# Retention attention and SwiGLU block on one core: first gate weight asked for ahead of the third pair's v, and first gate products ahead of the fourth pair's transposes

## The chip, the cores and the metric

The kernel runs on one core of a Trainium2 chip. The metric is the device time of one execution in microseconds (us). Three runs of the kernel before are shown, with their median. One more execution was profiled; its trace gives every duration used here, and the times in it count from the start of its span.

The engines are named as in the profile: PE (matrix products; PEld is its weight load), DVE (vector), ACT (scalar, activations), POOL (GpSimd) and SP, which here only asks for transfers. A "q" behind a name (SPq) is the sequencer of that engine.

## The reference

```python
def _attn_ref(q, k, v):                       # (8, 8, 576, 64): batch, head, position, head size
    scores = scale * np.matmul(q, k.transpose(0, 1, 3, 2))
    Dmat = np.where(rel >= 0, gamma[:, None, None] ** rel[None, :, :], 0.0)
    return np.matmul(scores * Dmat[None], v)

def _moe_ref(x, w_gate, w_val, w_out):        # x: (4608, 512), d_ff = 1536
    g = x @ w_gate
    return (g * (1.0 / (1.0 + np.exp(-g))) * (x @ w_val)) @ w_out
```

The attention's output, with the heads side by side, is x. All is in 32-bit floats on the chip; the three weights arrive as 64-bit floats.

## The kernel before, in words

**Attention by pairs.** Two heads of one batch are a pair, so there are 32 pairs; pairs 0 to 3 are the first batch. A pair is worked in chunks of 64 positions. Its steps are functions: `transposes` (line 455: PE turns k into `bankC` and q into `bankE`, ACT copies both out at line 467, and for pairs 2 and 3 POOL scales k at line 490), `scores` (547), `new_states` (522: products of k and v by chunk), `masked` (561: a list of ACT's copy `copies`, DVE's mask `own`, and the DVE steps `pairs`, `odd`, `evens` that add up the states), `own_values` (509), `earlier_values` (531: products of states and q, behind an empty instruction that waits for `own_values`) and `to_x` (598: for the first batch three ACT copies at line 625). `new_pair(i)` (777) is `scores`, `new_states`, and all of `masked`. `go_on(n)` and `part_on()` (839, 844) issue the next entries of `masked`.

**The first tile of tokens.** The first 512 positions of batch 0 make a first tile, `xs[0]`, with one group of 128 columns ("c") for each pair. `up0(f, chunks, parts)` (859) multiplies column block f of the weights (gate is part 0, value is part 1; f goes from 0 to 11) by the columns c of the tile. Blocks with an even f use `bankA` and `bankB`, those with an odd f `bankC` and `bankE`; when the last c is in, ACT applies Silu to the gate bank (line 874) and DVE multiplies (line 875), and only then may the bank be written for block f + 2. A product with c = 0 needs pair 0's output, c = 1 that of pair 1, and so on.

**The weights** come in 18 pieces. `load_w(m)` (368) asks for piece m; pieces 0 and 1 (first gate and first value piece) are asked for in halves of two transfers each, 256 KB a transfer. Pieces 0 to 4 are asked for on SP's queue, later ones (1024 KB each) on POOL's. `split(j)` (389) is two ACT instructions that take a half apart (lines 398 and 399), `rounding(j)` (408) two DVE instructions that put it together as 32-bit floats (lines 415 and 416). `split` asks for a later piece when its place comes free, so that POOL's transfers wait for ACT's line 399.

**The order** of each engine's work is written out by hand: the calls at the end of the kernel are the order of every queue. SP asks for transfers one after the other; each transfer uses one of eight semaphores in turn and waits for the one that had the same semaphore before. In the order before, SP asks for pair 2's q, k and v (`load(2)()`, line 325: v is what the second call asks for), then for the first half of the first gate and value piece (line 421), pair 3 (line 422), the second halves, pieces 2 and 3, and piece 4 when `held` is emptied. Then come the loads of pairs 4 and on, line 290 (k, v) and line 299 (eight transfers of 72 KB each of 128-byte rows, for q and k), one pair ahead of their use. From pair 4 on, q and k are turned by DVE at line 477, and ACT scales k at line 492.

Before `up0(0, [0], [0])`, the first gate product, stand 22 products of an identity matrix (line 1461) whose result nobody reads. Before them PE has `new_pair(2)` and `own_values(1)`; after it `earlier_values(1)`, the transposes of pair 3, and the products of c = 1 and of the value part.

## Time and profile before

| | us |
|---|---|
| three runs, median (lowest to highest) | 1014.41 (1012.95 to 1018.09) |
| the profiled execution's own time | 1013.87 |
| its span | 1012.2 |
| PE busy | 1005.7 (99%) |
| DVE busy | 713.4 (70%) |
| POOL busy | 571.9 (57%) |
| ACT busy | 286.4 (28%) |
| 16 DMA engines, mean of the core | 192 GB/s |

The rows of the profile read "start, duration, engine, line, operation, written tile<-read tiles"; in square brackets stands the idle time of the engine ahead of the row and what ended it. A matrix product in 32-bit floats is recorded as two passes, so that 22 products show as x44. [...] The chain of waits is followed back from the last instruction: at each step to whatever released it.

### The profile page before, as it was taken

How to read it: one execution, taken by the hardware profiler on the slowest of the kernel's cores; microseconds unless marked ns; L12 is line 12 of the kernel's file. 1: busy time of each engine (PE TensorE's matmuls, PEld its weight loads, DVE VectorE, ACT ScalarE, POOL GpSimd, SP SyncE). 2: the span in 40 equal slices, each digit the busy share in tenths (PEclk: the TensorE clock that was granted, in tenths of full speed). 3: DMA queues.
4: the chain of work that ended last, by engine and by line, in shares of the span. 5: the costliest groups of instructions: out<-in, count | busy, mean ns of one | idle time of the engine just before them, and what ended most of it. 6: DMA issues, size and time to landing. Idle time of an engine off the chain costs nothing.

```text
span 1012.2 us, 21328 instructions
## 1 busy us (share of the span) xinstructions
PE 1005.7 (99%) x8338; PEld 829.4 (82%) x8338; DVE 713.4 (70%) x1203; ACT 286.4 (28%) x636; POOL 571.9 (57%) x603
## 2 busy tenths in 40 slices
PE   9999999999999999999999999999999999999998
PEld 7655555888888888888888888888888888888887
DVE  5567988677875766977777678866575767566645
ACT  4644622131423312133322202233320012233110
POOL 3510458979475228575565157746672586566514
PEclk9999999999999999999999999999999999999999
DMA  9999986888788887757668686434454554445553
GB/s 242 280 265 258 201 236 230 222 236 217 182 209 215 215 213 215 195 157 197 180 183 225 176 203 197 152 131 161 162 173 141 154 189 147 146 155 184 179 161 103
DMA packets 273932, 194.44 MB, mean 192 GB/s; under 512 B 212328, under 2 KB 241896, under 8 KB 273832
## 3 DMA queue, kind: packets, MB, share of 16 engines
q1 hardware_dynamic: 248296, 94.77, 38.6%
q10 hardware_dynamic: 21360, 84.29, 25.5%
q0 software_dynamic: 4176, 14.03, 4.3%
q8 instruction: 66, 1.08, 0.5%
q14 instruction: 34, 0.28, 0.1%
HBM read 154.11 MB, written 38.93 MB: 191 GB/s over the span
## 4 chain that ended last, share of the span: by engine, by line
PE 90%; SPq 3%; DVE 2%; DMA 2%; issue 1%; POOL 1%; ACT 1%; ACTq 0%; DVEq 0%; POOLq 0%
PE bankC L1204 11%; PE bankB L1204 11%; PE bankA L1204 11%; PE bankE L1204 11%; PE bankB L1410 7%; PE bankE L1410 7%; PE bankC L1410 7%; PE bankA L1410 6%; SPq L299 2%; PE inner L1204 2%; PE outer L1204 2%; PE outer L517 2%; PE outer L544 1%; PE inner L558 1%; PE inner L528 1%
## 5 line engine op out<-in xcount | busy, mean ns | idle before, releaser
L1060 POOL TENSOR_TENSOR rest<-rest 128x512 f32<-128x512 f32 (+1 forms) x139 | 147.8, 1075 | 159.9 <-DVE rest L1060 112.5
L1219 POOL TENSOR_TENSOR arena<-rest,io 128x256 f32<-128x256 f32 x168 | 123.5, 746 | 89.9 <-ACT io L1218 89.3
L1218 ACT ACTIVATE io<-rest 128x256 f32<-128x256 f32 x192 | 79.2, 417 | 200.8 <-DVE rest L1060 138.9
L1204 PE MATMUL bankB<-rest,arena 128*128 128x256 f32 x448 | 114.9, 380 | 0.1
L1060 DVE TENSOR_TENSOR rest<-bankB,rest 128x512 f32<-128x512 f32 x116 | 78.6, 686 | 41.8 <-PE bankB L1204 30.0
L1204 PE MATMUL bankC<-rest,arena 128*128 128x256 f32 x416 | 106.3, 380 | 0.0
L1204 PE MATMUL bankA<-rest,arena 128*128 128x256 f32 x412 | 104.8, 379 | 0.0
L1060 DVE TENSOR_TENSOR rest<-bankA,rest 128x512 f32<-128x512 f32 x111 | 75.3, 686 | 38.4 <-PE bankA L1204 19.2
L1060 DVE TENSOR_TENSOR rest<-bankC,rest 128x512 f32<-128x512 f32 x110 | 74.6, 685 | 37.6 <-PE bankC L1204 26.6
L1060 DVE TENSOR_TENSOR rest<-bankE,rest 128x512 f32<-128x512 f32 x106 | 71.9, 686 | 36.5 <-PE bankE L1204 21.4
L1204 PE MATMUL bankE<-rest,arena 128*128 128x256 f32 x372 | 94.9, 380 | 0.0
L1204 PEld LDWEIGHTS bankB<-rest,arena 128*128 128x128 f32 x448 | 84.5, 190 | 12.8 <-POOL arena L1060 0.7
L1204 PEld LDWEIGHTS bankC<-rest,arena 128*128 128x128 f32 x416 | 78.5, 190 | 11.4 <-DVE rest L1060 0.8
L1204 PEld LDWEIGHTS bankA<-rest,arena 128*128 128x128 f32 x412 | 78.1, 190 | 10.8
L1204 PEld LDWEIGHTS bankE<-rest,arena 128*128 128x128 f32 x372 | 70.3, 190 | 10.1 <-DVE rest L1060 0.6
L1060 POOL TENSOR_TENSOR arena<-arena 128x256 f32<-128x256 f32 (+1 forms) x76 | 70.4, 950 | 8.1 <-PE bankC L1204 6.7
L1410 PE MATMUL bankB<-arena 128*128 128x256 f32 x264 | 61.0, 381 | 0.0
L1410 PE MATMUL bankE<-arena 128*128 128x256 f32 x264 | 60.8, 380 | 0.0
L1410 PEld LDWEIGHTS bankE<-arena 128*128 128x128 f32 x264 | 50.0, 190 | 6.9
L1410 PEld LDWEIGHTS bankB<-arena 128*128 128x128 f32 x264 | 49.8, 190 | 6.9
L1410 PE MATMUL bankC<-arena 128*128 128x256 f32 x240 | 55.2, 379 | 0.0
L1410 PE MATMUL bankA<-arena 128*128 128x256 f32 x228 | 52.5, 380 | 0.0
(291 smaller groups left out, 1875.3 us busy)
## 6 DMA issues: line engine op xcount, KB each, us to landing
arena<-up ACTq DMA_DIRECT2D x63, 896.0 KB, 4.8
arena<-dn ACTq DMA_DIRECT2D x65, 384.0 KB, 3.1
arena<-dn SPq DMA_DIRECT2D x39, 384.0 KB, 3.1
out_dram<-rest SPq DMA_DIRECT2D x31, 256.0 KB, 4.5
qk<-in_q_dram SPq DMA_DIRECT2D x108, 72.0 KB, 4.4
qk<-in_k_dram SPq DMA_DIRECT2D x108, 72.0 KB, 3.3
dn<-rest SPq DMA_DIRECT2D x26, 256.0 KB, 3.6
up<-arena SPq DMA_DIRECT2D x13, 512.0 KB, 4.8
```

Source lines behind the costliest of these rows:

```text
L299: queue.dma_start(out=qk[a * SQ : (a + 1) * SQ, n], in_=src[b, 2 * p + a // 2, :, (a % 2) * SQ : (a % 2 + 1) * SQ].rearrange("(j t) d -> t ...
L517: m = nc.tensor.matmul(value(i, hl, c), s["v"][rows, at], ret[rows, c % 2 if whole(i) else hl, c // 2], start=start, stop=start, skip_grou ...
L528: nc.tensor.matmul(z[half[hl], r, c], s["kn"][chunk(i, hl, 2 * c + r)], s["v"][rows, at], start=True, stop=True, skip_group_check=True)
L544: nc.tensor.matmul(xr[half[hl]] if c + 1 == NC else value(i, hl, c), state[half[hl], c, :], s["qT"][half[hl], ts(c, L)], start=False, stop ...
L558: nc.tensor.matmul(sc[chunk(i, hl, 2 * c + r)[0], r if whole(i) else hl, c], kT[half[hl], at], qT[half[hl], at], start=True, stop=True, sk ...
L1060: eng.tensor_tensor(out=out, in0=a, in1=b, op=ALU.add if sign > 0 else ALU.subtract)
L1204: m = nc.tensor.matmul(b[:, g * TB : (g + 1) * TB], w[:, g], x, start=(opens and g == 0), stop=True, skip_group_check=True)
L1218: nc.scalar.activation(out=s, in_=src[:, 0:TB], func=AF.Silu)
L1219: (nc.vector if busy and o != 2 and qd + 1 < NQ else nc.gpsimd).tensor_tensor(out=hid[:, qd, 2 * H + h, 2 * T + t], in0=src[:, TB : 2 * TB ...
L1410: nc.tensor.matmul(b[:, m * TB : (m + 1) * TB], lhs[:, qd, ts(m, P)], w[:, qd], start=(opens and qd == 0 and m == 0), stop=(qd == NQ - 1), ...
```

## The change

The request for pair 2's v is put behind the two transfers of the first half of the first gate piece. In the written order, `new_pair(2)` is taken apart: `own_values(1)` moves between `scores(2)` and `new_states(2)`, `earlier_values(1)` and `to_x(1)` come right after, then `split(1)` and `rounding(1)` ahead of the last entry of pair 2's mask list (`odd` and `evens`; `part_on()` has issued `pairs` by then). The products that nobody reads go from 22 to 3, the first gate products of c = 0 and c = 1 stand together, and the transposes of pair 3 come behind them.

```diff
@@ -322,7 +322,7 @@
     for f in values:
         f()
-    load(2)()
+    third = load(2)
@@ -419,6 +419,8 @@
     for m in range(2):
         load_w(m, (0,))
+        if m == 0:
+            third()
     load(3)()
@@ -1454,19 +1456,22 @@
     split(0)
     rounding(0, False)
     scale_run(3)
-    new_pair(2)
+    scores(2, True)
     own_values(1)
+    new_states(2)
+    earlier_values(1)
+    pieces.extend(masked(2))
+    go_on(2)
+    part_on()
+    to_x(1)[0]()
     split(1)
-    for _ in range(22):
+    rounding(1, False)
+    go_on(1)
+    for _ in range(3):
         nc.tensor.matmul(bankB[0:D, 0:D], ident[0:D, 0:D], ident[0:D, 0:D], start=True, stop=True)
-    up0(0, [0], [0])
-    earlier_values(1)
-    to_x(1)[0]()
-    put = transposes(3)
-    rounding(1, False)
-    for f in put:
+    up0(0, [0, 1], [0])
+    for f in transposes(3):
         f()
-    up0(0, [1], [0])
     up0(0, [0], [1])
     split(2)
     own_values(2)
```

## The prediction

> **What bounds the kernel now.** I read four views: the page, the timeline of the first 60 us, the chain of waits from 86 to 104 us, and who PE waited for.

> The page's busy times come first:

> ```profile
> PE 1005.7 (99%) x8338; PEld 829.4 (82%) x8338; DVE 713.4 (70%) x1203; ACT 286.4 (28%) x636; POOL 571.9 (57%) x603
> ```

> PE has no room left except at single places, so a change early on is worth what PE starts earlier, if PE is not made to wait again later. The timeline of the stage that is changed:

> ```profile
> 15.09 0.96 PE L528 MATMUL inner<-v,rest 64*64 64x64 f32 x32
> ...
> 16.20 0.67 ACT L398 ACTIVATE rest<-rest 128x512 f32<-128x512 f32 x1 [0.97 <-DMA rest<-in_moe_w_gate_dram]
> ...
> 16.30 2.73 PE L1461 MATMUL bankB<-ident 64*64 64x64 f32 x44
> ...
> 17.47 0.69 DVE L416 CUSTOM_DVE_ANT_0 arena<-arena,rest 128x1024 uint16<-128x1024 uint16 x1
> ...
> 18.96 1.13 PE L871 MATMUL bankA<-rest,arena 128*128 128x512 f32 x2
> ...
> 21.93 1.12 PE L871 MATMUL bankA<-rest,arena 128*128 128x512 f32 x2 [0.21 <-ACT rest L625]
> ```

> The reader is to see that ACT waited for the gate weight, that PE passed that time with unread products, and that these ran on until 18.96 although the weight was ready at 18.16 (17.47 + 0.69). Next, all of PE's waits for another engine:

> ```profile
> PE bankB L732 <- POOL ident masks.py:199: 1.6, 1, 1.6
> PE bankA L871 <- ACT io L874: 0.4, 1, 0.4
> PE inner L747 <- DVE kT L741: 0.3, 1, 0.3
> PE bankB L1204 <- ACT rest L1249: 0.2, 1, 0.2
> ```

> The second is the one that decides this case. It is at 102.36 us, and the chain of waits tells where it comes from:

> ```profile
> 84.68 2.69 SPq L299
> 87.37 0.05 issue
> 87.42 1.50 DMA qk<-in_k_dram
> ...
> 90.50 7.60 issue
> 98.11 0.68 ACT rest L398
> ...
> 101.83 0.49 ACT io L874
> 102.31 0.04 issue
> 102.36 1.98 PE bankA L871 x4
> ```

> PE has no slack there: it stood 0.38 us. ACT's Silu of block 8 frees bankA for block 10, and it stands in ACT's queue behind splits that waited 7.6 us for DVE. DVE in turn (its timeline) waited for a transfer, pair 7's k:

> ```profile
> 96.03 0.78 DVE L477 STREAM_TRANSPOSE kT<-qk 128x576 f32<-128x576 f32 x1 [3.45 <-DMA qk<-in_k_dram]
> ```

> **The change, step by step** (times of before; "to" is my estimate).

> 1. *Transfers.* By the trace's landing records, pair 2's v landed at 12.60 and 13.16, the gate's two transfers at 14.01 and 16.11. The last lost 1.2 us on one DMA engine only (15 of its 16 shares were in at 14.88), where a 16 KB instruction fetch sat from 13.12 to 14.31. Swapped, the same bytes run: the gate takes the first 512 KB of the 768, which were through ahead of that fetch, so it lands at about 14.0 (bounds: 13.7, and 15.1 if it still meets the fetch); v lands last, at 16.1 (bounds 14.9 and 16.2). Every later SP request keeps its place and its semaphore, so value, pair 3 and the rest land as before. This adds and removes no transfer.
> 2. *First rounding.* ACT is free at 15.23 (copy of line 775, 14.64 + 0.59), so the first split goes from 16.20 to 15.23; DVE's two instructions then end at 17.2, not 18.16.
> 3. *PE to the first gate product.* Scores of pair 2 start at 14.57 as before; `own_values(1)` follows at 15.3 (it waits for the same ACT copy); `new_states(2)` waits for v until 16.15 and issues for 0.5; `earlier_values(1)` 0.6; three unread products cost 3 x 2 x 58 ns = 0.35, the 19 removed had cost 2.2. First product: 17.65 instead of 18.96. In before, `new_states(2)` was through by 16.0; the later v costs it 0.6, and behind it on PE waits everything, so this is in the sum.
> 4. *c = 1 and transposes.* ACT's three copies (1.13) follow `earlier_values(1)` and end at 18.65: c = 1 goes from 21.93 to 18.7. Pair 3's transposes wait for its k (landed 19.50): 20.63 to 19.6. POOL's scaling behind them moves along.
> 5. *Value product.* ACT reaches `split(1)` at 18.65 (before 18.00), since the copies now stand ahead of it; DVE's rounding ends at 20.6 instead of 22.11, PE's product goes from 22.89 to 20.65. Behind this rounding on DVE now wait `odd` and `evens` (1.4 us): they end at 22.0 (before 20.95), and `earlier_values(2)` takes them at 22.2 (before 24.62). A wait added, but it ends together with PE's own work there.
> 6. *What is late next.* The value part of block 1 needs the weight transfer that landed at 25.34; two ACT and two DVE steps behind a landing took 3.0 us (25.35 to 28.36 less the 1.0 in which ACT was still at line 625): 27.35 against 29.20. From there PE's order and work are the same: own and earlier values of pair 3, then c = 2 at 30.6 instead of 32.50.

> Sum of the stage: **1.9 us** earlier (bounds: 1.0 if the gate meets the fetch and v is last, 2.2 as the unread products removed).

> **Where it goes.** From 20 to 62 us the DMA engines are full (in the table of stages their share is 1.04 to 1.35, where 1 is all 16 busy; more is records that overlap), and what SP asks for in that time is unchanged. So pair 5's k, whose landing at 62.3 starts DVE's line 477, can't come sooner by an earlier PE. From there DVE and ACT run without a pause into k of pair 6, the request for pair 7 waits for DVE's 77.47, and its k lands at 95.9. None of this waits for PE, so bankA is still freed at 102.3: PE comes 1.9 us sooner, stands 2.3 instead of 0.4, and the gain is gone. After 102.36 PE's work is the same. The likeliest shift is 0.

> **Rivals.**

> *The gain is kept* (shift -1.9, at most -2.3 with the 0.38 itself: 1012.0). It needs pair 7's k about 2 us sooner. For it: POOL's weight transfers wait for ACT's line 399, which moves with PE around 28 to 57 us, and the DMA share falls to 0.73 from 66 to 69 us and to 0.78 after 96, so there is some air in the loop. Against: the loop from 62.3 to 96.0 has DVE idle for transfers three times, 3.67, 0.48 and 3.45 us, and none for PE until 87.6.

> *Slower: POOL's bulk transfers overtake pair 5's k.* POOL's 1024 KB requests at 50.29, 50.99 and 57.37 move up with ACT by up to 1.9, while SP's 72 KB requests of 50.0 to 53.0 don't. The queues from 50 to 62 us:

> ```profile
> q0 software_dynamic: 679, 2.32, 64.1%
> q1 hardware_dynamic: 4936, 0.76, 55.2%
> ...
> qk<-in_k_dram SPq DMA_DIRECT2D x4, 72.0 KB, 10.3
> ```

> A 72 KB request that met two of POOL's took 10.3 us to land. If the third gets ahead of the rest too, pair 5's k lands 2.7 us later (1024 KB at the 380 GB/s of these slices), DVE's 62.34 becomes 65.0, and ACT's Silu of bankA at 67.77 becomes 70.5: PE, due at 69.1, is already back at 71.1 (before 70.98), and at 102.36 the loop is 2.2 to 3.5 late: 1016.1 to 1017.4. It decides if the third request gets ahead by over 0.3 us, since pair 5's last share landed just as that bulk began. [...]

> *The unread products were needed.* The first PE passes stood 213 ns apart until 6.4 us and 109 ns after, so PE ran at half speed while it was new to work, for 4.8 us. If PE fell back at 16 us, the 4.8 us that follow would lose 2.4, and the stage would gain nothing: time as in the likeliest case, since 102.36 binds. Against it: by step 3 PE stands 0.2 to 0.3 us at most. [...]

> **How the numbers follow.** The profiled execution took 1013.87 for its 1012.2 of span, 0.54 under the median of the runs shown; with a shift of 0 I take a value between the two, 1014.1. Chances: gain given back at 102.36 (shift -0.9 to +1) 0.48; kept, at least in half, 0.25; loop late 0.22; stage not faster 0.05, with the same time as the first. The range goes from the kept gain, 1013.87 - 2.3 = 1011.6, to the late loop, 1013.87 + 3.5 = 1017.4; the likeliest case alone is 1013.0 to 1015.2. About 0.5% (5.1 us) is what a measurement of this kernel can tell from no change; all three cases lie inside it. Beyond are a loop that falls a whole transfer further behind (0.08 slower) and one that gets more than I count (0.03 faster): same 0.89.

> **What would show it.** Right: ACT's first split at 15.2, first gate product near 17.7, c = 1 near 18.7, c = 2 near 30.6, DVE's line 477 still waiting at 62 and 96, and a PE wait of about 2.3 us for ACT's line 874 near 100. Wrong: v of pair 2 landing after 17, pair 5's k at 65 (loop late), or no PE wait before 104 with k of pair 7 landing by 94 (gain kept).

## The result, and the profile after

The changed kernel takes 1020.18 us (median of 6 executions, 1018.37 to 1022.61), the kernel before on the same chip 1014.2 us (6 executions). The ratio is 1.0056, with a 95% interval of 1.004 to 1.0071: **slower by 0.56%, some 5.7 us**. The forecast was no change, and the time lies above its range. The profiled execution took 1018.37 us with a span of 1016.7, so 4.5 us of span are to be found in the trace of before and after.

PE does the same work in the same busy time, in 38 passes less. This is the first line of the profile after:

```profile
PE 1005.2 (99%) x8300; PEld 828.6 (81%) x8300; DVE 712.1 (70%) x1203; ACT 286.3 (28%) x636; POOL 571.9 (56%) x603
```

The stage that was changed, in the timeline of after (start, duration, engine, line; line numbers are up to 5 higher than in before):

```profile
14.91 0.68 ACT L398 ACTIVATE rest<-rest 128x512 f32<-128x512 f32 x1
...
16.12 0.46 PE L519 MATMUL outer<-rest,v 64*64 64x64 f32 x16 [0.59 <-issue]
...
17.67 2.24 PE L873 MATMUL bankA<-rest,arena 128*128 128x512 f32 x4
...
21.01 1.12 PE L873 MATMUL bankB<-rest,arena 128*128 128x512 f32 x2 [0.22 <-DVE arena L416]
...
30.71 0.44 PE L519 MATMUL outer<-rest,v 64*64 64x64 f32 x10 [0.21 <-issue]
...
31.92 1.12 PE L873 MATMUL bankA<-rest,arena 128*128 128x512 f32 x2
```

The first gate product starts at 17.67 (18.96 before) and the value product at 21.01 (22.89), but c = 2 only at 31.92 (32.50): the lead of 1.3 to 1.9 us shrinks to 0.6. Two gaps in it say "issue": PE waited for nothing that the profile shows. What this is comes out below.

Then the waits of PE:

```profile
PE bankA L873 <- ACT io L876: 4.1, 1, 4.1
PE bankB L734 <- POOL ident masks.py:199: 1.6, 1, 1.6
PE outer L519 <- issue: 0.8, 2, 0.6
```

The first was 0.4 us at 102 us in before; now it is 4.1 us at the start of block 6. The timeline shows where it comes from, a row each of DVE, ACT, ACT and PE:

```profile
68.92 0.78 DVE L479 STREAM_TRANSPOSE kT<-qk 128x576 f32<-128x576 f32 x1 [10.25 <-DMA qk<-in_k_dram]
...
70.74 0.68 ACT L398 ACTIVATE rest<-rest 128x512 f32<-128x512 f32 x1 [14.26 <-DVE arena L415]
...
74.32 0.58 ACT L876 ACTIVATE io<-bankA 128x512 f32<-128x512 f32 x1
...
74.95 5.35 PE L873 MATMUL bankA<-rest,arena 128*128 128x512 f32 x8 [4.09 <-ACT io L876]
```

In before the same four stood here, the last without a wait:

```profile
62.34 0.78 DVE L477 STREAM_TRANSPOSE kT<-qk 128x576 f32<-128x576 f32 x1 [3.67 <-DMA qk<-in_k_dram]
...
64.17 0.69 ACT L398 ACTIVATE rest<-rest 128x512 f32<-128x512 f32 x1 [7.11 <-DVE arena L415]
...
67.77 0.59 ACT L874 ACTIVATE io<-bankA 128x512 f32<-128x512 f32 x1
...
70.98 3.70 PE L871 MATMUL bankA<-rest,arena 128*128 128x512 f32 x8
```

Pair 5's k was 6.6 us late, DVE's roundings behind it, ACT's splits behind those, and block 4's Silu behind the splits. The last row of after shows a second loss: the eight passes took 5.35 us where they took 3.70 before. The table by stages gives the granted clock (in each row the third number from the end):

```profile
70.90:74.90 4.00, 0.00 (x0) 0.00 (x0) 3.57 (x7) 3.94 (x8) 0.70 (x1) 1.00 0.63 102
74.90:78.30 3.40, 3.35 (x4) 1.51 (x5) 3.20 (x6) 3.32 (x7) 0.77 (x1) 0.50 0.94 291
78.30:81.70 3.40, 3.40 (x9) 1.52 (x8) 3.29 (x10) 1.88 (x4) 0.75 (x1) 1.00 1.14 314
```

PE stood for 4 us and then ran 3.4 us at half its clock. The transfers in between, 50 to 62 us, with the issues of k last (KB, and us to landing):

```profile
q0 software_dynamic: 782, 2.17, 65.1%
q1 hardware_dynamic: 5413, 0.92, 51.5%
...
qk<-in_k_dram SPq DMA_DIRECT2D x4, 72.0 KB, 11.7
```

SP's four requests for this k, first in before and then in after (start of the first, and from there to the end of the last):

```profile
50.02 2.99 SPq L299 DMA_DIRECT2D qk<-in_k_dram  x4
...
52.80 10.33 SPq L299 DMA_DIRECT2D qk<-in_k_dram  x4
```

The last of the four was begun at 51.99 in before and at 57.19 in after. POOL asked for its three 1024 KB transfers at 50.29, 50.99 and 57.37 in before, and at 52.81, 54.41 and 56.77 in after. So the third of them now stands ahead of k's last quarter, more because SP came later than because POOL came earlier.

So the span of after is before's, less 0.1 (PE's lead where its wait begins, at 70.86 against 70.98), plus 4.1 (the wait), plus 1.65 (the clock), less 1.1: at before's 102 us PE has come 0.6 nearer again (before's wait of 0.38 there is gone), and the rest follows in small steps.

### The profile page after: what moved, and what is told of

It reads as the page before. It is cut to its first block, busy times and chain, and to the rows that moved or that the text cites. A ratio compares the mean times of both kernels' runs of the same rounds, so it can differ in the third digit from the quotient of the medians.

```text
span 1016.7 us, 21254 instructions
## 1 busy us (share of the span) xinstructions
PE 1005.2 (99%) x8300; PEld 828.6 (81%) x8300; DVE 712.1 (70%) x1203; ACT 286.3 (28%) x636; POOL 571.9 (56%) x603
## 4 chain that ended last, share of the span: by engine, by line
PE 92%; SPq 3%; DMA 2%; ACT 1%; issue 1%; DVE 0%; ACTq 0%; DVEq 0%
PE bankC L1206 12%; PE bankB L1206 12%; PE bankA L1206 12%; PE bankE L1206 12%; PE bankB L1412 7%; PE bankE L1412 7%; PE bankC L1412 7%; PE bankA L1412 6%; SPq L299 2%; PE outer L519 2%; PE outer L1206 2%; PE inner L1206 2%; PE outer L546 1%; PE inner L560 1%; PE bankA L873 1%; PE inner L530 1%
## 5 line engine op out<-in xcount | busy, mean ns | idle before, releaser
L1412 PE MATMUL bankC<-arena 128*128 128x256 f32 x240 | 55.2, 379 | 0.0
```

The costliest lines, as they stand in the source:

```text
L1412: nc.tensor.matmul(b[:, m * TB : (m + 1) * TB], lhs[:, qd, ts(m, P)], w[:, qd], start=(opens and qd == 0 and m == 0), stop=(qd == NQ - 1), ...
```

## The experiments

The theories, in the order in which they came up: **A**, pair 5's k is late, and through DVE, ACT's splits and the Silu it holds PE at block 6. **B**, PE stands inside the scores near 126 us because a piece of its own program comes late; the change made that program 76 instructions shorter and put two waits in. **C** and **D** are guesses at what makes k late. This table has, for each kernel, PE's instructions against before, the ratio to before with its interval, and from its one profile: the start of DVE's transposition of pair 5's k, PE's waits at the starts of block 6 and of block 10, and the stall at PE's instruction 2753 (counted from 0 in the trace: weight loads, passes, waits). A profile shows one execution, and a ratio is that of six to twelve.

| kernel | PE instr. | ratio (95%) | k at | block 6 | block 10 | 2753 |
|---|---|---|---|---|---|---|
| before again | 0 | 0.9996 (0.9976 to 1.0016) | 63.38 | 0 | 2.55 | 0 |
| after again | -74 | 1.0045 (1.0025 to 1.0065) | 68.18 | 4.08 | 1.45 | 2.22 |
| swap alone | 0 | 0.9998 (0.9978 to 1.0019) | 66.38 | 0.44 | 1.48 | 0 |
| order alone | -74 | 1.0055 (1.0037 to 1.0074) | 67.16 | 2.93 | 1.03 | 2.21 |
| after, hold piece 9 | -74 | 1.0052 (1.0030 to 1.0074) | 64.31 | 1.03 | 0.83 | 2.21 |
| after, Silu first | -74 | 1.0053 (1.0035 to 1.0072) | 68.63 | 0.81 | 3.57 | 0 |
| after, 19 products more | +2 | 1.0031 (1.0014 to 1.0047) | 67.91 | 3.82 | 0 | 0 |
| both of these | +2 | 1.0011 (0.9989 to 1.0032) | 63.86 | 0 | 6.95 | 0 |
| before, 3 unread | -76 | 1.0053 (1.0035 to 1.0071) | 66.50 | 2.35 | 0.55 | 2.21 |
| after, piece 6 late | -74 | 1.0061 (1.0041 to 1.0081) | 66.71 | 3.93 | 0 | 1.94 |
| the same, 19 more | +2 | 1.0015 (1.0000 to 1.0029) | 66.48 | 2.65 | 0 | 0 |
| after, hold piece 5 | -74 | 1.0057 (1.0037 to 1.0077) | 67.69 | 4.09 | 1.35 | 2.22 |
| before, 3 wide | -76 | 1.0032 (1.0016 to 1.0049) | 67.55 | 2.71 | 0 | 2.22 |
| before, 22 on halves | 0 | 1.0021 (1.0008 to 1.0033) | 68.77 | 3.62 | 0 | 0 |
| after, 22 unread | +2 | 1.0008 (0.9994 to 1.0022) | 62.49 | 0 | 0.84 | 0 |
| piece 6 late, 19 more, Silu first | +2 | 1.0012 (0.9993 to 1.0031) | 67.53 | 0 | 5.99 | 0 |
| before, 67 on halves | +180 | 1.0048 (1.0030 to 1.0065) | 64.13 | 0 | 0 | 0 |
| before, 86 on halves | +256 | 1.0030 (1.0020 to 1.0040) | 62.52 | 0 | 0 | 0 |

### The two kernels again, and the parts of the change alone

The swap alone is the kernel before with these lines:

```diff
-    load(2)()
+    third = load(2)
...
         load_w(m, (0,))
+        if m == 0:
+            third()
```

The order alone is the changed kernel with `load(2)()` back in its old place; it has 3 unread products, as the changed kernel has.

> The kernel before, profiled once more. Theory (the three bulk weight transfers of GpSimd run as one block ahead of the fifth pair's k, DVE's transposition of that k comes 6.6 us late, and PE waits 4 us at block 6): the order of transfers of the first profile repeats, with two bulks, then k landing near 62, then the third bulk; time 1013 to 1015. Rival, a bad profile (the slow transfers of 20 to 26 us are the luck of one execution): this profile may as well show the slow stretch and k near 68, with a time near that of the first run of the kernel before.

> The changed kernel, profiled once more. Theory: k of the fifth pair lands near 68 to 69 again, PE waits near 4 us at block 6, the granted clock falls to 0.5 there, time 1018 to 1022. Rival, a bad profile: k lands near 62 in this one, and the 1020 of the median comes from somewhere else, for example from PE's first stage.

> Only the transfers change places (the third pair's v behind the first gate weight); PE, ACT and DVE keep the order of before. Theory: the time goes with the bulk block, whatever starts it; if the swap starts it (weights 20 to 45 us land later), k of the fifth pair lands near 68 and the time is 1018 to 1022; if not, k lands near 62 and the time is 1013 to 1016. Rival, the loss is in PE's stage because the third pair's v comes late: PE loses about 1 us ahead of the second pair's values, the time is 1015 to 1016, and k of the fifth pair stays near 62.

> Only the order of PE, ACT and DVE changes; the third pair's v is asked for where it was. Theory: as for the swap alone, the time is read off k of the fifth pair: near 68 gives 1018 to 1022, near 62 gives 1013 to 1016. Rival, the loss is in PE's stage through the late v: no loss here, 1012 to 1014, with the first gate product near 18 and the gain of the stage kept until block 6.

The late k repeats after the change (68.18, block 6 held 4.08 us) and not before it (63.38). The second profile of before is of its slowest execution, 1018.18 us, and shows where before itself can lose: at block 10, behind block 8's Silu, with the granted clock at half for 3.41 us from 104.14 on (the eight passes take 3.60 us at full clock):

```profile
104.59 5.16 PE L871 MATMUL bankA<-rest,arena 128*128 128x512 f32 x8 [2.55 <-ACT io L874]
```

So a wait at block 10 alone tells nothing of the change. The slower transfers from 20 to 26 us repeat in before (1.56 MB there, 1.62 and 1.57 in after; the execution that the prediction was made from had 1.97), with k at 63.38 all the same, so they alone are not the cause. The swap alone changes nothing that can be measured, and its k at 66.38 cost PE only 0.44 us. The order alone, with its 3 unread products, has the whole loss, also without any late v, so the rival of the late v is out. Its waits:

```profile
PE bankA L871 <- ACT io L874: 4.0, 2, 2.9
PE inner L558 <- issue: 2.2, 1, 2.2
PE bankB L732 <- POOL ident masks.py:199: 1.6, 1, 1.6
PE outer L517 <- issue: 0.9, 1, 0.9
```

The second was not in the first profile after (the fastest of its six executions), and it is in "after again" at the very same instruction, 2753, in the middle of a run of equal passes. The stall of line 517 is instruction 961, that of after's line 519 at 16.12 is 449; 449, 961 and 2753 lie multiples of 256 apart. The trace records transfers of 16,384 bytes on a queue of kind "instruction", 66 for PE's 16,961 instructions in before, which is one for each 256, so I take them for pieces of PE's program. In "order alone" one of them ran from 123.40 to 124.77, PE stopped at 123.80 and went on at 126.01. Of its 66 borders two show in PE's waits as idle time of the kind "issue", 0.9 us at 961 and 2.2 us at this one; the other 64 show none of 0.2 us or more. This made theory B.

### Theories A and B taken away one at a time

Piece 9 held:

```diff
+        if m == 9:
+            wait = nc.gpsimd.nop()
+            tc.add_manual_dep(wait.ins, turned[-1].ins.name, ...)   # DVE's transposition of pair 5's k
```

> The changed kernel, with the third bulk weight transfer of GpSimd (piece 9) asked for only after DVE has transposed k of the fifth pair. Theory A (the bulk block delays k): DVE transposes k at 62 to 65.5, PE waits at most 0.5 us at block 6, the clock stays full there; as PE is early again, part of it comes back as a wait near 102 us; 1015.5 to 1017.5 if the stall of 2.2 us inside the scores near 126 us stays, less if not. Rival (k is late for another reason: SP's own requests come late): transposition still at 67 to 69, time 1019 to 1022.

k came at 64.31 and block 6 waited 1.03 us at full clock, near what theory A has, but the time stayed at 1.0052 (1019.89 us, not 1015.5 to 1017.5): the next loads were late in turn (pair 6's k at 84.32, against 77.47 in before and 83.50 in after), and PE waited 1.09 us at 85.5, 1.41 at 90.1 and 0.83 at 105.0, besides the 2.21 of theory B. The wait was moved, not removed.

Block 4's Silu ahead of the splits:

```diff
+        if f == 4:
+            plan.append(lambda: up0(4, range(HP)))
         round_until({4: 12, 6: 13, 8: 14, 9: 15, 10: 16, 11: 17}.get(f, f + 2))
...
-        plan.append(lambda f=f: up0(f, range(HP)))
+        if f != 4:
+            plan.append(lambda f=f: up0(f, range(HP)))
```

> The changed kernel, with block 4's Silu and product ahead of the eight splits and roundings of pieces 12 and 13 in the order of ACT and DVE. Transfers are asked for as they were, so k of the fifth pair stays late (67 to 69). Theory A (PE loses its time through the chain k, transposition, split, Silu of block 4): PE doesn't wait at block 6 any more, the clock stays full there, 1015.5 to 1018, with a wait near 102 us. Rival (PE is held by the weights or by k itself): the wait at block 6 stays over 3 us, or moves to the next block, and the time stays at 1019 to 1022.

k was late (68.63) and block 6 waited 0.81 us and not 4, so the chain is the one named. But the time did not fall: the waits of this kernel,

```profile
PE bankA L873 <- ACT io L876: 3.6, 1, 3.6
PE outer L519 <- issue: 2.0, 2, 1.3
PE bankB L734 <- POOL ident masks.py:199: 1.6, 1, 1.6
PE bankB L873 <- DVE arena L416: 0.9, 1, 0.9
```

put the 3.6 us at block 10 now (107.5 us), behind block 8's Silu and the same roundings, with the clock at half for 6.83 us. My 1015.5 to 1018 was wrong (1019.55).

Nineteen products more, alone and with the Silu first:

```diff
+    for n in range(19):
+        nc.tensor.matmul(bankB[half[n % 2], 0:D], ident[half[n % 2], 0:D], ident[half[n % 2], 0:D], start=True, stop=True)
```

> The changed kernel, with 19 more unread products in the place of those that the change removed, but on alternate halves of the array, so that they cost some 1.2 us and not 2.2. They give PE's program the length of before. Theory B (PE stands 2.2 us inside the scores near 126 us because a 16 KB piece of its own program comes late; the 76 instructions that the change removed moved the borders of these pieces into a dense stretch): this stall and the clock's fall behind it are gone, the time falls by 2.5 to 4 us against the changed kernel, to 1016 to 1017.5; the wait at block 6 stays. Rival (the stall belongs to the late transfers, not to the length of the program): it stays, and the time is that of the changed kernel or 1 us more.

> Both of the last two edits together. Theories A and B: both losses are gone, 1012 to 1014.5, no wait at block 6, no stall near 126 us. If only one of the two theories holds: 1015.5 to 1018. If neither: 1019 to 1022.

With the 76 instructions back, the passes that were cut in two run through:

```profile
124.42 0.63 PE L560 MATMUL inner<-qT,kT 64*64 64x64 f32 x30
```

The wait at block 6 stayed at 3.82 us. The ratio 1.0031 is lower than the changed kernel's 1.0056, with intervals that still overlap; the time was 1018.17 us, above my 1016 to 1017.5. Together with the Silu it is 1.0011, no longer told from before. This isn't the clean end of both losses that the table's two zeros suggest: the profile is of the slowest of the twelve executions, 1023.25 us, and in it PE stood 6.95 us at block 10 and the clock was at half for 10.24 us.

### The unread products alone, and two guesses at the late k

```diff
-    for _ in range(22):
+    for _ in range(3):
         nc.tensor.matmul(bankB[0:D, 0:D], ident[0:D, 0:D], ident[0:D, 0:D], start=True, stop=True)
```

> The kernel before with 3 unread products in the place of 22 and nothing else: PE's program is 76 instructions shorter, as in the changed kernel, and the order of work is that of before. Theory B (the borders of PE's 16 KB program pieces move into a dense stretch): PE stands about 2.2 us at its instruction 2753, inside the scores near 122 us, the clock falls to 0.5 for 3.4 us behind it, and the time is 1016 to 1018.5. Rival (the late transfers make that stall, the length of the program doesn't): no such stall, 1013 to 1014.5.

This is the run that decides: the kernel before, with nothing changed but 19 products that nobody reads left out, is at 1.0053, **the whole loss of the change**. Its timeline:

```profile
122.14 0.52 PE L558 MATMUL inner<-qT,kT 64*64 64x64 f32 x21
124.87 0.35 PE L558 MATMUL inner<-qT,kT 64*64 64x64 f32 x9 [2.21 <-issue]
125.14 1.28 PE L882 MATMUL bankA<-rest,arena 128*128 128x512 f32 x2
126.22 1.91 PE L882 MATMUL bankB<-rest,arena 128*128 128x512 f32 x2
```

The stall cuts the 30 passes in two. In before they run through:

```profile
120.44 0.63 PE L558 MATMUL inner<-qT,kT 64*64 64x64 f32 x30
```

Behind the stall the granted clock is 0.50 for 3.41 us, and pairs of passes that take 1.02 us take 1.91. (In before's trace each pass of 512 columns is recorded with 0.59 us and the next starts 0.43 us behind its start, so a row can end behind the start of the next one.) The time, 1020.06 us, was more than I expected (1016 to 1018.5), since the late k came with it (66.50, block 6 held 2.35).

Piece 6 behind the small transfers (with `held` for j = 5, emptied behind `end_loads()`), piece 5 held until PE's `own_values(3)`, and the first with the 19 products:

> The changed kernel, with GpSimd's weight transfer of piece 6 asked for behind its twenty small transfers (end_loads) and not ahead of them; nothing needs piece 6 before 62 us. Theory A, narrowed (k of the fifth pair is late because GpSimd's small transfers stand behind the landing of piece 6, so that the queues run dry at 43 to 47 us): GpSimd's wait of 4 to 5 us goes, the transfers from 42 to 50 us move 1.3 MB or more (0.95 to 1.1 in the changed kernel), k is transposed at 62 to 65.5, PE waits under 1 us at block 6; 1016 to 1018, with theory B's stall still there. Rival (k is late because of the bulk weight transfers behind, whenever the small ones run): transposition at 67 to 69, 1019 to 1021.

> The last edit and the 19 padding products together. Theories A and B: neither the wait at block 6 nor the stall near 126 us, 1012 to 1014.5. B alone: as with the padding alone, 1017 to 1018.5.

> The changed kernel, with GpSimd's weight transfer of piece 5 held until PE's own values of the fourth pair are done (near 30.5 us, against 27.6). Theory C (the sixteen DMA engines get out of step because piece 5 runs beside SyncE's piece 4, which then lands over 5 us after its first share): piece 4 lands by 35, its shares lie within 2.5 us, and k of the fifth pair is transposed 1 to 3 us earlier, 65 to 67; 1017 to 1019.5. Rival (the shares are apart for another reason): piece 4 at 37 to 38 as before, k at 67 to 69, 1019 to 1021.

Both guesses fall. With piece 6 late, 1.96 MB moved from 42 to 50 us (0.96 in after), and k still came at 66.71. With piece 5 held, piece 4 landed at 34.91 and no longer at 38.24, and k came at 67.69. The padding again took the stall and most of the loss (1.0061 to 1.0015, intervals apart), but not the wait at block 6 (2.65 us), and the time, 1016.29 us, is above the 1012 to 1014.5 that both theories together gave.

### Number of instructions and time of PE parted

Three wide products take the time of the 22 (2.84 us on the trace against 2.73) in 76 instructions fewer; 22 on alternate halves are the same number in 1.50 us.

```diff
-    for _ in range(22):
-        nc.tensor.matmul(bankB[0:D, 0:D], ident[0:D, 0:D], ident[0:D, 0:D], start=True, stop=True)
+    for _ in range(3):                                            # 3 wide
+        nc.tensor.matmul(bankB, ident, early[0][:, 0:512], start=True, stop=True)
...
+    for n in range(22):                                           # 22 on halves
+        nc.tensor.matmul(bankB[half[n % 2], 0:D], ident[half[n % 2], 0:D], ident[half[n % 2], 0:D], start=True, stop=True)
```

> The kernel before with its 22 small unread products replaced by 3 of 512 columns: they take PE nearly the same time (3 x 2 x 0.43 = 2.6 us against 2.7), in 76 instructions fewer. It parts the two things that the removal of 19 products changes. Theory B (number of instructions): the stall of 2.2 us at PE's instruction 2753 is there, with the clock's fall, 1016.5 to 1018.5. If the late k of the fifth pair comes from PE being early (theory D): k is transposed at 62 to 64.5 as in the kernel before and PE doesn't wait over 0.5 us at block 6. If it comes from the number of instructions too (program pieces that are fetched at other times): k at 66 to 69 and 1019.5 to 1021.5.

> The kernel before with its 22 unread products on alternate halves of the array: the same number of instructions in about half the time. Theory B: no stall at PE's instruction 2753. Theory D (PE early makes the chain through k late or uncovers it): PE waits 1 to 3 us at block 6, 1014.5 to 1017. If time doesn't matter, only the number of instructions: 1012.5 to 1014.5.

> The changed kernel with all 22 unread products as they were: only the order of the work and of the transfers is changed, and PE's program is as long as before. If the reduction from 22 to 3 is the whole loss (theory B with its part of theory A): 1013 to 1015.5, no stall near 126 us, k of the fifth pair at 62 to 66.5. If the order has a loss of its own: 1016 to 1019, with k at 67 to 69 and a wait over 2 us at block 6.

> The changed kernel with the 19 padding products, piece 6 asked for behind GpSimd's small transfers, and block 4's Silu ahead of the splits. Theory A (what is left after the padding is the chain k, split, Silu of block 4): no wait at block 6, 1012 to 1014. Rival (the wait moves to block 10 near 104 us and takes as much): 1015 to 1017.

Fewer instructions in the same time: 1.0032. The same number in less time: 1.0021. Both at once (3 unread): 1.0053, which is their sum, though each has an interval of 0.0013 to 0.0018 to either side. These are rows of the one with 3 wide products:

```profile
73.58 5.40 PE L871 MATMUL bankA<-rest,arena 128*128 128x512 f32 x8 [2.71 <-ACT io L874]
...
126.80 0.35 PE L558 MATMUL inner<-qT,kT 64*64 64x64 f32 x9 [2.22 <-issue]
```

It has both losses although its first gate product starts at 18.89, as in before (18.96): theory D (k is late because PE is early) doesn't explain that. So the 1.0032 isn't the price of the stall alone. And this is the one with 22 on halves, without the stall and with the wait, PE being only 0.5 us early (18.49). Its time, 1016.88 us, is what theory D gave; its wait is longer than D's 1 to 3 us:

```profile
PE bankA L871 <- ACT io L874: 3.6, 1, 3.6
PE bankB L732 <- POOL ident masks.py:199: 1.6, 1, 1.6
PE inner L528 <- issue: 0.7, 2, 0.3
```

Piece 6 late with the padding and the Silu first gave 1.0012 and no wait at block 6 with k at 67.53, but its profiled execution, the slowest of twelve, stood 6.0 us at block 10: the rival's move of the wait, in some executions.

The changed order with all 22 products is at 1.0008 (0.9994 to 1.0022): the order of work and of transfers, about which the prediction argued, neither costs nor gains what can be measured, though the interval leaves room for a loss of 2.2 us. Its median, 1015.82 us, is just above my 1013 to 1015.5. Its block 6 runs as in before:

```profile
70.61 3.70 PE L873 MATMUL bankA<-rest,arena 128*128 128x512 f32 x8
```

### The place of the border or the number of instructions

The last edit with 67 and with 86 products for 22.

> The kernel before with 67 unread products on alternate halves in the place of its 22: 180 instructions more, so that the borders (every 256 instructions in the profiles) lie with respect to the scores as they do in the changed kernel (76 fewer, and 76 + 180 = 256). PE's products come some 1.9 us later. Theory B in its sharp form (the place of the border decides, not the number of instructions): PE stands about 2.2 us at instruction 3009, inside the same scores, the clock falls behind it, 1017 to 1020. Rival (a shorter program is what hurts): no such stall, 1014 to 1016.5.

> The kernel before with 86 unread products on alternate halves: 256 instructions more, so that every border lies where it lay in the kernel before. PE's products come some 3.2 us later than before. Theory B: no stall inside the scores, 1014 to 1017.2 (at most the 3.2 us of PE). Rival (more instructions hurt by themselves): a stall as with 67, 1018 to 1021.

With 86 the loss is 3.0 us (ratio 1.0030), less than PE's later start (3.9 us at the first gate product, 22.9, and still 3.9 at block 6), and nothing is left for a stall. With 67 PE starts 1.6 us sooner than with 86 and the time is longer, 1.0048, though the intervals overlap. The times lean to the sharp form of theory B; the profile doesn't show it: the profiled execution, the fastest of six, has no stall at 3009 (its piece was fetched from 116.13, ahead of PE's border at 120.52). The six times fall into two groups, 1016.83 to 1017.74 and 1020.21 to 1021.25, some 3.5 us apart. A stall of 2.2 us with a clock loss of 1.65 would give this distance, but so would a wait at block 10 with its clock loss, as in "before again", and one of the upper three (1020.21) has a mean granted clock of 1.0, so no such clock loss. No profile was taken of the upper group, and the cause of its time isn't shown.

No version beat the kernel before; the nearest are the changed order with 22 products and the two padded kernels with the Silu first, which can't be told from it.

## Why the prediction was wrong, point by point

- *Transfers (step 1).* Right: v at 16.11 (16.1). The gate came at 13.60, still sooner than 14.0. That value, pair 3 and the rest "land as before" was wrong from 22.8 on: the weights landed 0.6 to 3.6 us later in this profile; in the second profile of before, too, pieces 2 to 4 came 1.0 to 2.8 us later.
- *Rounding, first product, c = 1, transposes (2 to 4).* Right within 0.3 us: split 14.91 (15.23), first product 17.67 (17.65), c = 1 at 18.8 (18.7), transposes 19.75 (19.6). What I charged to v in step 3 was in part a border of PE's program: 0.59 us of the kind "issue" at instruction 449 (16.12), with v landing at 16.11, and it is there again in "after, 19 products more".
- *Value product (5).* 21.01 for 20.65.
- *Late next (6).* The weight landed at 25.94 and not at 25.34, block 1's value part came at 28.02 for 27.35, and c = 2 at 31.92 for 30.6: a gain of 0.6 us and not 1.9.
- *The removed products.* The step that failed first. They were costed at their time on PE, "the 19 removed had cost 2.2", and at nothing as instructions. As instructions they are worth 3.2 us (1.0032 at equal time, interval 1.0016 to 1.0049; that kernel's profile has the stall of 2.22 us and a late k as well): "After 102.36 PE's work is the same" was true of the work and not of the program's borders. I had the evidence in hand, the 16 KB instruction fetch that I used in step 1 to explain a late share.
- *Pair 5's k still landing at 62.3.* The second failed step. It came at 66.4 to 68.9 in most kernels of the table. "What SP asks for in that time is unchanged" was true of the list and not of the times: SP's last request for this k came 5.2 us later in after (57.19 for 51.99). The rival "POOL's bulk transfers overtake pair 5's k" had the right outcome for after's profile (POOL's third transfer ahead of k's last quarter) and the right place (PE at block 6). But it had POOL moving up by up to 1.9 us, where POOL's third request moved up by 0.6 and SP's fell back; k was late by 6.6 us and not 2.7, and the fall of the clock behind the wait (1.65 us) wasn't priced. The step from k to PE holds in every profile in which PE waited for that Silu with the order unchanged there: block 6 starts 6.0 to 6.1 us behind DVE's start on k (68.92 to 74.95, 67.16 to 73.19, 66.50 to 72.53, 68.77 to 74.80). By that, as my estimate, k may come up to 65 without harm where PE is as early as in before (70.98 less 6.0).
- *"The unread products were needed"* was nearly dismissed, with 0.05, for the clock at 16 us. They were needed, for another reason.
- *Gain kept, and given back at 102.36.* Neither: PE was 5.05 us late there (107.41).

What stays open: why k of pair 5 comes at 62 to 64 in some kernels and at 66 to 69 in others. Holding piece 9 moved it to 64.31, with one profile; piece 5 and piece 6 are not the answer (theory C falls), and PE's lead alone isn't either ("before, 3 wide" has none). The traces show one thing that goes with it. Where POOL's transfers kept their places (piece 9 not held, piece 6 not late), k came at 62.3 to 64.1 in the six profiles in which SP's last request for it was begun by 54.41 (both of before, "after, 22 unread", "both of these", and 67 and 86 on halves), and at 66.4 to 68.9 in the nine in which it was begun from 54.76 on; "before, 3 unread" (54.13, k at 66.50) is the one exception. What makes SP late wasn't tested. Two profiles of one kernel differ by up to 1.0 us in it, and 22 products on halves, with PE 0.5 us early, are slower than before by 1.0021 (1.0008 to 1.0033) in a way that I can't derive. What also stays open is why a program piece is sometimes fetched early enough.

## What to carry to other kernels

Count instructions as well as time: where PE ran over 256 short instructions in 2.0 us ("before, 3 unread"), a border of its program inside that run went with a stall of 1.94 to 2.22 us in seven of the nine profiles with the shorter program, and with a fall of the clock behind it in three of the seven. Leaving out 19 products that nobody reads, over 100 us ahead, had moved this border by 76 instructions. So before an order is blamed for a change of some us, run the same edit with the number of PE's instructions kept. A wait on a chain of loads that is only hidden by a few us (here k may come until 65, by the estimate above) may come back at the next link when it is taken away at one: with block 4's Silu first, 0.8 us were left at block 6 and 3.6 us came at block 10.

## What the runs showed of the hardware

**Program pieces.** In the twenty profiles PE's idle times of over 0.15 us of the kind "issue" lie at instructions 449, 705, 961 and 2753, and further back at 5825, 6081, 7617, 7873, 11201 and 11457, each 193 more than a multiple of 256. A single one, of 0.42 us at 2916 in "after, 22 unread", lies elsewhere. In "before, 3 unread" PE passed border 2497 at 120.44; the next piece was fetched from 122.03 to 123.37, and PE, at the end of its piece at 122.66, went on at 124.87: 4.4 us from one border to the next piece, and 1.5 us from its landing. There the 256 instructions took 2.0 us; in before the borders near are 8.9 us apart (111.18, 120.09, 129.01), and none stalls. Of the nine profiles with the shorter program (the table's eight and the first one of after), seven stall at 2753, for 1.94 to 2.22 us, and in three of the seven the clock falls behind it ("after again", "order alone", "before, 3 unread"); of the nine with the old length (eight and the first one of before), none stalls there.
